# Copies of sampled keys on the activation engine, and a planner that counts on VectorE being held by GpSimd

## The chip, the cores and the metric

The kernel runs on one core of a Trainium2 chip. The engines work in parallel, each through its own queue of instructions in order, and wait for each other by semaphores: TensorE (PE, products), VectorE (DVE), ScalarE (ACT, the activation engine), GpSimd (POOL) and SyncE (SP, which here issues every transfer). On-chip data lies in SBUF (128 partitions) or in PSUM, where products land. The metric is the device time of one execution in microseconds; runs of the same kernel are given by their median.

## What is computed

Block-sparse attention, then a feed-forward layer with a rational function in its middle, cut from the reference:

```python
# q, k, v: (4, 8, 768, 64); 24 blocks of 32 rows; 3 sampled blocks of keys per query block
mask = np.abs(blk_i - blk_j) <= 1                      # the block and its neighbours
mask |= (blk_i == 0) | (blk_j == 0) | (blk_i == 23) | (blk_j == 23)
for qb in range(24):
    for kb in sampled_blocks[qb]:
        mask[qb*32:(qb+1)*32, kb*32:(kb+1)*32] = True
attn = softmax(where(mask, q @ k.T / 8, -1e9)); x = attn @ v      # (3072, 512)
h = x @ w_in                                                      # (3072, 2048)
P = a[0] + a[1]*h + a[2]*h*h + a[3]*h*h*h
Q = 1 + abs(b[0])*abs(h) + abs(b[1])*h*h
out = (P / (Q + 1e-6)) @ w_out                                    # (3072, 512)
```

So 22 of 24 query blocks look at eight blocks of keys (three neighbours, three sampled, the two edges), and the first and the last look at all. The weights come as 64-bit floats.

## The kernel before

**Tiles.** A query block with its eight heads is one step of attention. Keys and queries are scaled by a power of two and split into two halves of 16 bits, a high one (`high`, line 632 for keys) and a low one (`low`, VectorE, line 378), transposed on TensorE (line 660) and copied out of PSUM. For the first batch of the four the transposed keys of all 24 blocks stay in SBUF, in `kall`. For the later ones they go to a scratch in DRAM and come back by transfers, block by block.

**One step of attention.** Scores on TensorE (line 876), maxima with the mask's bias on VectorE (886), the negated maximum (915), exponentials on ScalarE (904), four transposes of the result (945), their copy out of PSUM (147, `pT`), products with the values (1002). Values come by transfers (lines 964 to 972). In the first batch the eight blocks of keys of a query block must lie side by side: the three neighbours are a slice of `kall`, and the two edge blocks (line 1072, once) and the three sampled ones (line 829, 128x256 elements each) are copied into one of two buffers `kxs`. The sampled blocks' numbers are data, so each step loads them into registers first (line 768). Before the change all of this copying is on GpSimd, three copies a step in 22 steps.

**The feed-forward part.** Groups of 256 rows (8 query blocks), and in them 16 units of two quarters of 128 columns. Per unit: first products on TensorE (lines 1113 to 1115), three ScalarE instructions that read PSUM (1120, 1124, 1134), VectorE's rational function (1127 to 1158) with ScalarE's logarithm and exponential in its middle (1141, 1144), second products (1169 to 1171).

**Decoding the weights.** In the first quarter of the program the 64-bit weights are loaded in 32 pieces (lines 422, 425). Each is converted (151 on GpSimd or 147 on ScalarE), packed by three VectorE instructions over SBUF (434, 437, 440), and then split into a high and a low part: input weights by ScalarE and GpSimd (`dw`, then line 498), output weights by ScalarE or GpSimd and GpSimd (line 451).

**The order.** All steps are entered in a list as `Op`s with an engine, a price in ns, the steps that they come after, and a priority. `issue` (lines 161 to 266) is a list scheduler that runs while the kernel is built: it keeps a modelled time `now` for each engine, takes the `Op` that could start first, and writes its instructions. So prices and starting rules set the order of every engine's queue, and nothing is reordered on the chip. An `Op` made with `among` names a home engine and may name others; another engine is taken if it could start earlier by more than `other[e]` (500 ns for VectorE, 534 for ScalarE, 243 for GpSimd). Where TensorE would wait long early in the program, `issue` writes filler products (line 159). The lines of the starting rule are these:

```python
196                    t = max([now[e], o.at[e]] + [s.ring.free[0][0] for s in o.takes])
197                    if e == SY:
198                        t = max(t, lanes[0])
199                    key = (max(t - slack, now[e]) + (0 if e == o.engs[0] else other[e]), o.prio, o.n)
```

Of the kernel before, what the change touches and what calls it, by code (L numbers as in the profile page):

```python
# [23 lines left out]
def kernel(  # L24
# [27 lines left out]
    nc = tc.nc  # L52
# [46 lines left out]
    OWN = {VE: 127, SC: 143, PO: 96}  # L99
    MARGIN = 17.0  # L100

    class Ring:


# [56 lines left out]
    def issue(ahead):  # L161
        def work_of(t, price, share):
            for x in (int(t / 3413), int(t / 3413) + 1):
                busy[x] = busy.get(x, 0.0) + share * max(0.0, min(t + price, (x + 1) * 3413) - max(t, x * 3413))

        def tick(t):
            nonlocal window, warm
            while window < int(t / 3413):
                share = busy.pop(window, 0.0) / 3413
                warm, window = share > (0.45 if warm else 0.85), window + 1  # L170

        todo = {e: [] for e in (VE, SC, PO, TE, SY, None)}
        now = dict.fromkeys(todo, 500.0)
        clock, dma, lanes = -1.0, 0.0, [0.0] * 8
        busy, window, warm = {}, 0, False
        for n, o in enumerate(plan):
            o.n, o.wait = n, len(o.after) + (o.behind is not None)
            for a in o.after:
                a.next.append(o)
            if o.behind:  # L180
                o.behind.next.append(o)
            if not o.wait:
                for e in o.engs:
                    todo[e].append(o)
        left = len(plan)
        fsh = 0.8
        other = {VE: 500, SC: 534.0, PO: 243.0}
        unit_of = {VE: nc.vector, SC: nc.scalar, PO: nc.gpsimd}
        slack, fend, f00, fgap = 21.0, 80000, 3000, 0
        while left:  # L190
            best = None
            for e, l in todo.items():
                for o in l:
                    if o.prio > clock + ahead or not all(s.ring.free for s in o.takes):
                        continue
                    t = max([now[e], o.at[e]] + [s.ring.free[0][0] for s in o.takes])
                    if e == SY:
                        t = max(t, lanes[0])
                    key = (max(t - slack, now[e]) + (0 if e == o.engs[0] else other[e]), o.prio, o.n)
                    if best is None or key < best[0]:  # L200
                        best = key, t, o, e
            if best is None:
                lim = [o for l in todo.values() for o in l]
                raise AssertionError([(o.eng, o.prio, o.run.__qualname__, [len(s.ring.free) for s in o.takes]) for o in lim][:40] + [clock])
            _, t, o, o.eng = best
            e = o.eng
            for x in o.engs:
                todo[x].remove(o)
            for s in o.takes:
                s.buf = s.ring.free.pop(0)[1]  # L210
            price = o.alt[e] if o.alt else o.price() if callable(o.price) else o.price
            o.start = t
            if isinstance(price, list):
                for ns, size in price:
                    t = max(t, lanes.pop(0) if e == SY else t) + ns
                    dma = max(dma, t + 650) + size / 225.0
                    if e == SY:
                        lanes.append(dma + 900)
                end = dma + 900
            elif e == TE:  # L220
                f0 = max(now[e], f00)
                while f0 < fend:
                    tick(f0)
                    f = 213 if warm else 427
                    if f0 + f + fgap > t:
                        break
                    fill()
                    work_of(f0, f, 1.0)
                    f0 += f
                tick(t)  # L230
                if now[e] < fend:
                    w = window
                    x0 = w * 3413
                    for _ in range(2):
                        if not warm or t - x0 < 700 or busy.get(w, 0.0) >= fsh * (t - x0):
                            break
                        fill()
                        work_of(t, 213, 1.0)
                        t += 213
                if not warm:  # L240
                    price *= 2 if price > 1100 or price < 500 else 1.8
                work_of(t, price, o.work)
                end = t = t + price
            else:
                end = t = t + price
            now[e] = t
            o.end = end
            o.run(unit_of[e]) if o.alt else o.run()
            if o.unit is not None:
                clock = max(clock, o.unit)  # L250
            for s in o.uses:
                s.left -= 1
                s.end = max(s.end, end + (0 if isinstance(price, list) else 200))
                if not s.left:
                    s.ring.free.append((s.end, s.buf))
                    s.ring.free.sort(key=lambda f: f[0])
            for x in o.next:
                if x.behind is not o:
                    for y in x.engs:
                        lat = MARGIN if isinstance(price, list) else OWN.get(e, 0) if y == e else LAT.get((e, y), 160) + MARGIN  # L260
                        x.at[y] = max(x.at[y], end + lat)
                x.wait -= 1
                if not x.wait:
                    for y in x.engs:
                        todo[y].append(x)
            left -= 1
# [348 lines left out]
    def rest(b, w, j, d, o_scale, sc, prio, before):  # L615
        first = b == 0
        t, g = units[j]
# [18 lines left out]
        def low():  # L636
            split16(d["ld"], sc[0], d["hl"], w, None)

        o = Op(among("k", PO, po=671, ve=396, sc=613) if w == 0 else among("K", PO, po=914, ve=600), 0, high, [o_scale, o_ld], prio, takes=[s_hl], uses=[s_ld])
        o = Op(VE, 663 if w == 0 else 800, low, [o], prio, uses=[s_ld, s_hl])  # L640
        if w == 1:
            def store():
# [153 lines left out]
    def attention(b, j, prio):  # L796
# [15 lines left out]
        for m, x in enumerate(xs):  # L812
            def one(m, x):
# [6 lines left out]
                if near and n > 1:  # L820
                    deps += [o for t in range(NCH) for o in k_evac[b, t]]
                    kslots = s_kall
                elif near:
                    s_kx = Slot(r_kx)

                    def copies():
                        rows = sampled_rows(x, mybir.EngineType.Pool)
                        for r in range(NR):
                            nc.gpsimd.tensor_copy(out=kxs[:, s_kx.buf, r].rearrange("p h r -> p (h r)"), in_=kall[:, bass.ds(rows[r], 1)].rearrange("p o h r -> p (o h r)"))

                    a = Op(PO, 1500, copies, [o_setup, chain["edges"]], p - 1, takes=[s_kx], uses=s_kall)
                    deps.append(a)
                    kslots = [s_kx] + s_kall
                else:
                    s_kg = Slot(r_kg)

                    def load():
                        kg, ks, = kgs[s_kg.buf], kv[b][0]
                        flat = kg.rearrange("p s h r -> p s (h r)")
                        if n > 1:  # L840
                            nc.sync.dma_start(out=flat, in_=ks[m * NS:(m + 1) * NS].rearrange("b p c -> p b c"))
                            return
                        nc.sync.dma_start(out=flat[:, 0:3], in_=ks[i - 1:i + 2].rearrange("b p c -> p b c"))
                        if h["new"]:
                            nc.sync.dma_start(out=flat[:, 3 + NR:], in_=ks[0:NB:NB - 1].rearrange("b p c -> p b c"))
                        rows = sampled_rows(x)
                        for r in range(NR):
                            nc.sync.dma_start(out=flat[:, 3 + r], in_=ks[bass.ds(rows[r], 1)].rearrange("o p c -> p (o c)"))

                    def price():  # L850
                        h["new"] = fresh("k", x, s_kg)
                        if n > 1:
                            return [(475, 524288)]
                        l = [(475, 196608)] + ([(475, 131072)] if h["new"] else [])
                        return l + [(860, 65536), (560, 65536), (560, 65536)]

                    a = Op(SY, price, load, [o_setup] + k_done[b], p - 1.95, takes=[s_kg], uses=[s_scr[b]], behind=chain.get("kg"))
                    chain["kg"] = a
                    deps.append(a)
                    kslots = [s_kg]  # L860
# [458 lines left out]
```

## Time and profile before

| | |
|---|---|
| median of 3 runs | 892.88 us (891.15 to 894.04) |
| the profiled execution | 894.15 us |
| its span, first to last instruction | 892.0 us |
| TensorE busy | 828.4 us (93%), 10328 products |
| VectorE busy | 743.9 us (83%), 1824 instructions |
| ScalarE busy | 653.1 us (73%), 1379 instructions |
| GpSimd busy | 157.0 us (18%), 188 instructions |
| DMA, one queue | 146.29 MB, 65.8% of 16 engines' span |

The profile is of one execution. A line such as L829 is a line of the kernel as it is printed above. "Busy" is the union of an engine's instructions; an engine's waits for semaphores, its register work and its transfers' issues aren't in it. The stage table gives busy time for each engine in a stretch of the span, with TensorE's granted clock (1.00 is full) and the share of time in which the 16 DMA engines were busy. GpSimd's spans are rough.

### The profile page before, as it was taken

To read this page: it belongs to the slowest core of one execution; us is meant where nothing else is said; L and a number is where in the kernel's file an instruction comes from. 1 tells how busy PE (TensorE), PEld (TensorE's weight loads), DVE (VectorE), ACT (ScalarE), POOL (GpSimd) and SP (SyncE) were. 2 spreads that over 40 slices of the span, in tenths; PEclk is the share of its full clock that TensorE was granted. 3 is DMA by queue.
4 is the path that set the end of the run, shared out by engine and by line. 5 is a ranking of instruction groups with operands and counts; after the bars stand their busy time and mean duration, and the time that the engine had idled before them with its cause. 6 is when DMAs were issued, how large, how long until landed. Compare 5 with 4: busy or idle time off the path is not lost.

```text
span 892.0 us, 27246 instructions
## 1 busy us (share of the span) xinstructions
PE 828.4 (93%) x10328; PEld 644.8 (72%) x10328; DVE 743.9 (83%) x1824; ACT 653.1 (73%) x1379; POOL 157.0 (18%) x188
## 2 busy tenths in 40 slices
PE   8988586776999999989999999999999999999997
PEld 3555365565778888777887788878888787788885
DVE  5668999979999888869877788988888887788885
ACT  6668666794788787778876887798758587767563
POOL 2434755736420000100000000200000000000000
PEclk9999798688899999999999999999999999999999
DMA  7799788875776976589655975699557556740000
GB/s 204 188 180 219 175 185 172 183 203 161 188 175 160 250 211 155 149 201 240 176 144 149 264 203 161 156 236 240 152 151 183 145 158 161 174 113 25 1 25 24
DMA packets 238482, 148.02 MB, mean 166 GB/s; under 512 B 16016, under 2 KB 222736, under 8 KB 238352
## 3 DMA queue, kind: packets, MB, share of 16 engines
q1 hardware_dynamic: 238352, 146.29, 65.8%
q8 instruction: 82, 1.34, 0.7%
q14 instruction: 48, 0.39, 0.2%
HBM read 128.92 MB, written 11.01 MB: 157 GB/s over the span
## 4 chain that ended last, share of the span: by engine, by line
PE 61%; DVE 8%; ACT 3%; DMA 3%; SPq 2%; issue 1%; ACTq 0%; DVEq 0%
PE ph L1113 8%; PE acc L1169 8%; PE acc L1171 8%; PE acc L1170 8%; PE ph L1114 7%; PE ph L1115 7%; PE av L1002 5%; PE pt L945 4%; PE sp L876 4%; DMA ld<-in_k_dram 1%; DVE gh L1148 1%; DVE ab L1137 1%; PE sp L733 1%; DVE tt L1154 1%; PE sp L1048 1%
## 5 line engine op out<-in xcount | busy, mean ns | idle before, releaser
L1113 PE MATMUL ph<-xh,wi 128*128 128x256 f16 x768 | 213.2, 278 | 3.8 <-DVE tt L1130 2.6
L1115 PE MATMUL ph<-xh,wi 128*128 128x256 f16 x768 | 212.0, 276 | 2.4 <-POOL wi L498 2.4
L1114 PE MATMUL ph<-xl,wi 128*128 128x256 f16 x768 | 212.0, 276 | 1.0 <-DVE xl L1060 1.0
L904 ACT ACTIVATE pr<-pr,st,cq 128x256 f32<-128x256 f32 x224 | 132.2, 593 | 61.0 <-DVE st L915 54.2
L1169 PE MATMUL acc<-wo_h,gh 128*128 128x512 f32 x384 | 164.9, 429 | 0.0
L1171 PE MATMUL acc<-wo_h,gl 128*128 128x512 f32 x384 | 154.7, 403 | 7.3 <-DVE gl L1158 6.6
L1170 PE MATMUL acc<-wo_l,gh 128*128 128x512 f32 x384 | 154.1, 401 | 1.2 <-POOL wo_l L451 1.2
L1120 ACT ACTIVATE sq<-ph,fc 128x512 f32<-128x512 f32 x96 | 65.3, 680 | 60.2 <-PE ph L1115 59.7
L1137 DVE SCALAR_TENSOR_TENSOR ab<-sq,absb,ab 128x512 f32<-128x512 f32 x96 | 74.1, 772 | 34.3 <-ACT ab L1134 34.0
L151 POOL TENSOR_SCALAR hlq<-ldq,scq 128x512 f16<-128x512 f32 x24 | 23.2, 968 | 445.2 <-DVE scq L352 239.5
L1113 PEld LDWEIGHTS <-wi 128*128 128x128 f16 x768 | 76.2, 99 | 32.2 <-issue 16.5
L886 DVE CUSTOM_DVE_ANT_1 pr<-sp,bias 128x256 f32<-128x256 f32 x224 | 84.6, 418 | 13.8 <-PE sp L876 13.4
L1171 PEld LDWEIGHTS acc<-wo_h,gl 128*128 128x128 f32 x384 | 73.6, 192 | 26.6 <-DVE gl L1158 9.3
L1148 DVE SCALAR_TENSOR_TENSOR gh<-tt,par,rr 128x512 fp32r<-128x512 f32 x96 | 74.9, 780 | 17.1 <-PE acc L1170 13.1
L945 PE MATMUL pt<-ident,pr 128*128 128x128 f32 x448 | 77.1, 294 | 11.8 <-ACT pr L904 7.7
L1115 PEld LDWEIGHTS <-wi 128*128 128x128 f16 x768 | 76.1, 99 | 13.8 <-POOL wi L498 2.9
L1169 PEld LDWEIGHTS acc<-wo_h,gh 128*128 128x128 f32 x384 | 73.9, 192 | 15.7 <-issue 1.2
L945 PEld LDWEIGHTS pt<-ident,pr 128*128 128x128 f32 x448 | 67.4, 206 | 24.7 <-ACT pr L904 10.1
L1170 PEld LDWEIGHTS acc<-wo_l,gh 128*128 128x128 f32 x384 | 73.9, 192 | 14.0 <-POOL wo_l L451 1.8
L1114 PEld LDWEIGHTS <-wi 128*128 128x128 f16 x768 | 76.1, 99 | 9.1 <-issue 1.1
L1002 PE MATMUL av<-vg,pT 128*32 128x64 f32 x3584 | 75.1, 226 | 4.7 <-ACT pT L147 2.5
L1002 PEld LDWEIGHTS av<-vg,pT 128*32 128x32 f32 x3584 | 57.1, 112 | 29.5 <-issue 8.9
(140 smaller groups left out, 1669.3 us busy)
## 6 DMA issues: line engine op xcount, KB each, us to landing
vg<-in_v_dram SPq DMA_DIRECT2D x312, 64.0 KB, 3.3
vg<-in_v_dram SPq DMA_DIRECT2D x88, 192.0 KB, 4.1
vg<-in_v_dram SPq DMA_DIRECT2D x24, 512.0 KB, 5.2
kall<-ks SPq DMA_DIRECT2D x52, 192.0 KB, 2.9
kall<-ks SPq DMA_DIRECT2D x156, 64.0 KB, 2.0
ld<-in_k_dram SPq DMA_DIRECT2D x36, 256.0 KB, 5.5
wl<-in_moe_w_in_dram SPq DMA_DIRECT2D x32, 256.0 KB, 4.8
wl<-in_moe_w_out_dram SPq DMA_DIRECT2D x16, 512.0 KB, 4.1
```

The costliest lines, as they stand in the source:

```text
L886: nc.vector.tensor_tensor_reduce(out=prs[x][:, g].rearrange("p (s r) -> p s r", r=BLK), in0=h["sp"][:, g].rearrange("p (s r) -> p s r", r= ...
L904: nc.scalar.activation(out=prs[x][:, g], in_=prs[x][:, g], func=AF.Exp, scale=Q["c"], bias=st[:, 6 + g:7 + g], accum_out=total if n == 1 e ...
L945: nc.tensor.transpose(pp[:, jj * P:(jj + 1) * P], cols, ident)
L1002: nc.tensor.matmul(av[rows, g], pT[:, 2 * g + kt, rows] if plain else pT[:, 2 * g + kt, pa_, rows], vf[:, g * HG + h4, kt * D:(kt + 1) * D ...
L1113: nc.tensor.matmul(o, wh, xh[:, :, cc], start=(cc == 0), stop=False)
L1114: nc.tensor.matmul(o, wh, xl[:, :, cc], start=False, stop=False)
L1115: nc.tensor.matmul(o, wl, xh[:, :, cc], start=False, stop=(cc == NCC - 1))
L1137: nc.vector.scalar_tensor_tensor(out=d["ab"], in0=d["sq"], scalar=absb[:, 1:2], in1=d["ab"], op0=ALU.mult, op1=ALU.add)
L1148: nc.vector.scalar_tensor_tensor(out=d["gh"], in0=d["tt"], scalar=par[:, 0:1], in1=d["rr"], op0=ALU.add, op1=ALU.mult)
L1169: nc.tensor.matmul(acc[:, t], ghs, wo_h[:, f], start=(new and e == 0), stop=False)
L1170: nc.tensor.matmul(acc[:, t], ghs, wo_l[:, f], start=False, stop=False)
L1171: nc.tensor.matmul(acc[:, t], gls, wo_h[:, f], start=False, stop=(last and e == 1))
```

## The change

Three things change. The three copies of sampled keys of a step, and the register loads ahead of them, move from GpSimd to ScalarE, with a price of 1100 ns in place of 1500. The high halves of keys (`high`, for keys of all batches) have ScalarE as home, and GpSimd and VectorE as the others. And the planner notes, after each `Op` on GpSimd, its modelled start and end in `held`; a VectorE `Op` that would start in between, and whose function isn't one of a list of those that read PSUM, starts later by half of what is left.

```diff
+    READS_PSUM = {"maxima", "cubic3", "weigh", "evac_high", "evac_low", "largest", "add", "copy", "evac", "whole"}
+    HELD = 0.5
...
+        held = 0.0, 0.0
...
+                    if e == VE and held[0] <= t < held[1] and o.run.__name__ not in READS_PSUM:
+                        t += HELD * (held[1] - t)
                     key = (max(t - slack, now[e]) + (0 if e == o.engs[0] else other[e]), o.prio, o.n)
...
             now[e] = t
+            if e == PO:
+                held = o.start, end
...
-        o = Op(among("k", PO, po=671, ve=396, sc=613) if w == 0 else among("K", PO, po=914, ve=600), 0, high, [o_scale, o_ld], prio, takes=[s_hl], uses=[s_ld])
+        o = Op(among("k", SC, po=671, ve=396, sc=613) if w == 0 else among("K", PO, po=914, ve=600), 0, high, [o_scale, o_ld], prio, takes=[s_hl], uses=[s_ld])
...
-                        rows = sampled_rows(x, mybir.EngineType.Pool)
+                        rows = sampled_rows(x, mybir.EngineType.Activation)
                         for r in range(NR):
-                            nc.gpsimd.tensor_copy(out=kxs[:, s_kx.buf, r]..., in_=kall[:, bass.ds(rows[r], 1)]...)
-
-                    a = Op(PO, 1500, copies, [o_setup, chain["edges"]], p - 1, takes=[s_kx], uses=s_kall)
+                            nc.scalar.copy(out=kxs[:, s_kx.buf, r]..., in_=kall[:, bass.ds(rows[r], 1)]...)
+
+                    a = Op(SC, 1100, copies, [o_setup, chain["edges"]], p - 1, takes=[s_kx], uses=s_kall)
```

What it does to the queues shows at two places. The first is ScalarE's queue at the first sampled blocks, where exponentials (`pr`) follow each other with the query's evacuation (`qa`) and the evacuations of transposed results (`pT`) between them. Line numbers of the changed kernel are 3 to 8 higher (904 is 912, 147 is 150, 737 is 745, 829 is 837). Before:

```order
L904 ACTIVATE pr,sm<-pr,st,cq 128x256 x2
L147 ACTIVATE wi<-wl 128x512
L147 ACTIVATE pT<-pt 128x512
L904 ACTIVATE pr,sm<-pr,st,cq 128x256 x2
L737 ACTIVATE qa<-sp 128x2x512
```

The same place now, from the second block's last copy:

```order
L837 COPY kx<-kall 128x256
L776 TENSOR_LOAD ix
L837 ISA
L837 COPY kx<-kall 128x256
...
L745 ACTIVATE qa<-sp 128x2x512
L912 ACTIVATE pr,sm<-pr,st,cq 128x256 x4
L776 TENSOR_LOAD ix
L837 ISA
L837 COPY kx<-kall 128x256
```

Each block now brings a register load, three register instructions (`ISA`) and three copies into this queue; the third block's stand ahead of the evacuation of the query and of the first exponentials, and the fourth's behind four exponentials instead of beside two.

The second is GpSimd's queue at the first group of input weights: `wi<-wl` is the conversion of a piece, `dw<-wi` its scaling and `wi<-dw,wi` its low part, `hlq` a query's high half. Before, from the last copies that stand ahead of the group's scaling:

```order
L768 TENSOR_LOAD ix
L829 ISA
L829 COPY kx<-kall 128x256
...
L151 TENSOR_SCALAR dw<-wi,scw 128x512 x3
L498 TENSOR_TENSOR wi<-dw,wi 128x512 x3
L151 TENSOR_SCALAR dw<-wi,scw 128x512
```

Now, from the copies of the two edge blocks, which stay on GpSimd:

```order
L1080 COPY kx<-kall 128x512 x2
L154 TENSOR_SCALAR hlq<-ldq,scq 128x8x64
L154 TENSOR_SCALAR wi<-wl 128x512 x4
L154 TENSOR_SCALAR dw<-wi,scw 128x512 x3
L506 TENSOR_TENSOR wi<-dw,wi 128x512 x3
```

The decode of this group follows the edge blocks' copies at once, with all four conversions on GpSimd, where 13 blocks of copies stood between.

## Rows read from the trace of the kernel before

**Rows 1.** Stage table: busy us and count by engine, clock, DMA share, GB/s

```profile
27.00:82.00 55.00, 47.48 (x902) 28.49 (x901) 38.12 (x138) 37.20 (x97) 28.62 (x53) 0.97 0.91 192
82.00:104.00 22.00, 13.87 (x240) 10.09 (x237) 18.81 (x44) 17.79 (x41) 13.94 (x16) 0.95 0.99 239
104.00:201.00 97.00, 73.92 (x985) 56.80 (x986) 88.31 (x194) 71.45 (x153) 51.58 (x56) 0.82 0.78 180
201.00:258.00 57.00, 48.01 (x558) 36.67 (x557) 56.97 (x123) 35.89 (x71) 29.24 (x23) 0.88 0.70 176
258.00:892.00 634.00, 621.99 (x7516) 501.68 (x7514) 525.12 (x1270) 474.52 (x983) 26.38 (x27) 1.00 0.61 157
```

**Rows 2.** Timeline, GpSimd and VectorE: start us, duration us, engine, line, operation

```profile
92.08 2.82 POOL L498 TENSOR_TENSOR wi<-dw,wi 128x512 f16<-128x512 f32 x2 [1.21 <-ACT wi L147]
97.90 3.20 POOL L498 TENSOR_TENSOR wi<-dw,wi 128x512 f16<-128x512 f32 x2
101.08 1.13 POOL L151 TENSOR_SCALAR hlq<-ldq,scq 128x512 f16<-128x512 f32 x1
...
92.36 1.53 DVE L437 SCALAR_TENSOR_TENSOR dw<-wl,dw 128x512 int32<-128x512 int32 x1
...
100.01 0.14 DVE L724 TENSOR_SCALAR cq<-cq 128x1 f32<-128x1 f32 x1
...
101.64 0.73 DVE L1130 SCALAR_TENSOR_TENSOR tt<-ph,fc,tt 128x512 f32<-128x512 f32 x1
...
112.77 0.69 DVE L437 SCALAR_TENSOR_TENSOR dw<-wl,dw 128x512 int32<-128x512 int32 x1
```

**Rows 3.** One line's or tile's instructions: ns min/median/max, waits (us, times)

```profile
L829 POOL COPY kx<-kall x66: 392/400/952, 27.3 to 182.3; 128x256 f16 x66
...
  PE sp L876: 11.1, 8
...
L768 POOLq TENSOR_LOAD <-ix x22: 725/730/946, 26.2 to 175.3; - x22
```

**Rows 4.** Stage table for the tile `kx`: TensorE's reads, then GpSimd's copies

```profile
104.00:201.00 97.00, 5.58 (x144) 15.16 (x24) 0.82 0.78 180
```

**Rows 5.** Timeline of VectorE, instructions that run beside copies and high halves

```profile
102.30 0.80 DVE L1154 SCALAR_TENSOR_TENSOR tt<-tt,par,ab 128x512 f32<-128x512 f32 x1
...
129.97 0.88 DVE L1127 TENSOR_TENSOR tt<-tt,sq 128x512 f32<-128x512 f32 x1
...
153.28 1.17 DVE L378 SCALAR_TENSOR_TENSOR hl<-ld,sc,hl 128x512 f16<-128x512 f32 x1 [0.59 <-POOL hl L151]
...
179.10 1.06 DVE L1151 SCALAR_TENSOR_TENSOR ab<-ab,gh 128x512 f32<-128x512 f32 x1
...
182.78 0.62 DVE L434 TENSOR_SCALAR wi<-wi 128x512 int32<-128x512 int32 x1
```

**Rows 6.** Groups of TensorE: busy us, mean ns, idle before and its releaser

```profile
L1115 PE MATMUL ph<-xh,wi 128*128 128x256 f16 x768 | 212.0, 276 | 2.4 <-POOL wi L498 2.4
...
L159 PE MATMUL acc<-ident 128*128 128x512 f16 x180 | 49.1, 401 | 1.7 <-DVE ident L93 1.7
```

**Rows 7.** Groups of ScalarE up to 290 us

```profile
L904 ACT ACTIVATE pr<-pr,st,cq 128x256 f32<-128x256 f32 x70 | 41.3, 593 | 19.7 <-DVE st L915 19.6
...
L297 ACT ACTIVATE absb<-par 128x2 f32<-128x2 f32 x1 | 0.2, 204 | 3.9 <-DMA par<-in_moe_b_dram 3.9
```

**Rows 8.** Timeline of GpSimd at the first sampled blocks

```profile
27.35 2.27 POOL L829 COPY kx<-kall 128x256 f16 x6
```

**Rows 9.** Groups of GpSimd up to 290 us

```profile
L451 POOL TENSOR_TENSOR wo_l<-dw,wo_h 128x512 fp32r<-128x512 f32 x16 | 23.4, 1461 | 18.3 <-ACT wo_h L147 17.8
L498 POOL TENSOR_TENSOR wi<-dw,wi 128x512 f16<-128x512 f32 x16 | 22.7, 1436 | 4.7 <-ACT wi L147 4.7
```

**Rows 10.** Transfers issued: count, KB each, median us to landing

```profile
vg<-in_v_dram SPq DMA_DIRECT2D x312, 64.0 KB, 3.3
vg<-in_v_dram SPq DMA_DIRECT2D x88, 192.0 KB, 4.1
```

More of the change, by code (lines that the diff above doesn't have):

```diff
@@ L826, in copies @@
                     def copies():
-                        rows = sampled_rows(x, mybir.EngineType.Pool)
+                        rows = sampled_rows(x, mybir.EngineType.Activation)
                         for r in range(NR):
-                            nc.gpsimd.tensor_copy(out=kxs[:, s_kx.buf, r].rearrange("p h r -> p (h r)"), in_=kall[:, bass.ds(rows[r], 1)].rearrange("p o h r -> p (o h r)"))
-                    a = Op(PO, 1500, copies, [o_setup, chain["edges"]], p - 1, takes=[s_kx], uses=s_kall)
+                            nc.scalar.copy(out=kxs[:, s_kx.buf, r].rearrange("p h r -> p (h r)"), in_=kall[:, bass.ds(rows[r], 1)].rearrange("p o h r -> p (o h r)"))
+                    a = Op(SC, 1100, copies, [o_setup, chain["edges"]], p - 1, takes=[s_kx], uses=s_kall)
                     deps.append(a)
```

## The prediction

> **What bounds the kernel now.** I started from the page's busy shares (TensorE 93%, VectorE 83%, ScalarE 73%), but they are averages over stages with different limits, so the stage table is the view that counts [rows 1]. It shows four regimes. From 27 to 104 us the DMA engines are 91% and 99% busy: transfers set the pace. From 104 to 201 us VectorE is busy 88.31 of 97 us and ScalarE 71.45. From 201 to 258 us VectorE is busy 56.97 of 57 us. From 258 us to the end TensorE is busy 621.99 of 634 us, at the full clock. The copies of the change lie in the first 201 us. They can move the end only by bringing the start of the last regime forward or back: from about the 42nd first-layer half on (lines 1113 to 1115), TensorE's orders before and after agree but for a few swaps.
>
> So the question is how long the prelude lasts, and in its part from 104 to 258 us VectorE is the scarce engine. Some of its busy time is no work. Beside GpSimd's 2.82 us of line 498 an instruction of line 437, with two inputs in SBUF, is recorded at 1.53 us; without GpSimd it takes 0.69 [rows 2]. One that reads PSUM, line 1130, keeps its 0.73 us while GpSimd's line 151 runs [rows 2].
>
> **The change, part by part.**
>
> *Key copies leave GpSimd.* They are 66, at a median of 400 ns [rows 3], in 22 blocks of three; 15.16 us of them lie from 104 to 201 us [rows 4]. What VectorE gets back is not that time but only the holding. I went through the VectorE instructions that overlap such a copy and took from each the usual duration of its line where GpSimd is silent. From 82 to 201 us there are 16, the first at 102.30 and the last at 182.78; a typical one, line 1127 at 129.97, takes 0.88 us [rows 5], 0.19 more than the 0.69 of such a width. Together they lose 2.6 us. Holds before 82 us lie in the transfer-bound stage and count nothing. **Term 1: -2.6 us.**
>
> *High halves of keys.* The planner may now put them on ScalarE first. Of 24, GpSimd did 23; it keeps 13, ScalarE has 10 and VectorE one. Two VectorE instructions in the prelude were held by one, 1.17 us at 153.28 and 1.06 at 179.10 [rows 5]; against 0.69 alone [rows 2] that is 0.85. **Term 2: -0.8 us.** In exchange VectorE gets one high half and one weight conversion. Neither shows on VectorE before; the nearest row is line 434, of the same width, 0.62 us beside a copy [rows 5]. Between nothing (in the transfer-bound stage) and 1.5 us I take two at 0.4. **Term 3: +0.8 us.**
>
> *GpSimd's queue gets shorter.* TensorE stands idle 2.4 us in front of line 1115 for GpSimd's line 498 [rows 6]. Without copies ahead of it this comes sooner, but TensorE isn't the scarce engine there: from 0 to 2.4 us, and I take a fifth. **Term 4: -0.5 us.**
>
> *Copies arrive on ScalarE.* The trace has no ScalarE copy of 128x256. It lies above an instruction of 2 elements, 204 ns, and below one of 256 with its exponential, 593 ns [rows 7]. Half-way is 0.4 us, so three make 1.2 and 22 blocks 26 us (13 to 39). Ten high halves instead of one, less three copies of weights that leave ScalarE, are six more at the 0.6 of [rows 7], 4 us. Together 30 us. ScalarE's idle time from 27 to 201 us is 174 - 126.4 = 47.6 us [rows 1], so the load fits and leaves 17. Each block also loads three indices into registers, 730 ns on GpSimd's queue [rows 3]. There they were hidden: six copies with such a load between them took 2.27 us, 0.38 apiece [rows 8]. If ScalarE hides none, 22 x 0.73 = 16 us more, and its slack is gone. I take hidden, as the queue that was seen did it.
>
> In sentences by themselves: the Trainium skill ("DMA: Bandwidth & Descriptors", Latency and other measured facts) gives loads of this kind a floor of about 600 ns. Unhidden, that is an estimated 13 us of ScalarE, and speaks against the change; the row's 730 ns is longer, and decides.
>
> ScalarE's queue also takes over a wait. The copies of a block wait for the scores that used its buffer two blocks earlier; GpSimd stood 11.1 us in 8 such waits [rows 3]. Behind them on ScalarE are queued the query's evacuation (line 737), exponentials (904) and evacuations before the value product (147); TensorE's transposes and VectorE's sums wait for those. 15 of the 22 blocks stand before the first output product, most of them in the transfer-bound stage, which covers them; ScalarE waits 19.6 us for line 915 as it is [rows 7], and copies fill part of that. From 0 to 11 us, and I take the low end. **Term 5: +0.5 us.**
>
> *The planner's new rule.* In the plan a VectorE instruction over SBUF starts later by half of what is left of GpSimd's instruction, so that one over PSUM may go first. Most holding comes from lines 451 and 498, 1.46 and 1.44 us long [rows 9], and they stay on GpSimd. I looked for the rule's effect in the new order: of the six instructions behind each of the 16 output-weight decodes (line 440), 40 of 96 read PSUM before and 29 of 96 now. The plan doesn't do there what the rule is for. **Term 6: 0 us**, with some 4 on either side.
>
> *More filler.* 201 warm-up products of line 159 in place of 180, which took 49.1 us [rows 6]. They stand at the start, where TensorE waits for transfers, so they cost nothing; with real work behind all 21 it would be 21 x 0.27 = 6 us.
>
> **Sum.** -2.6 - 0.8 + 0.8 - 0.5 + 0.5 + 0 = -2.6; the small holds that I left out (under 0.04 us each) bring it to about -3. The profiled execution took 894.15 us, 2.15 more than its span of 892.0; it becomes 891.15. The median of the runs, 892.88, lies 1.27 lower, so the forecast is **889.9 us**, -0.3%.
>
> **Rivals.**
>
> *ScalarE's queue becomes the bound (slower).* Place: the sampled blocks from 104 to 201 us, where ScalarE is busy 71.45 of 97 [rows 1]. Seven blocks (8.4 us), their register loads (5.1) and six halves (3.6) bring it to 88.6, as full as VectorE. From there neither engine has slack: each wait at the head of ScalarE's queue delays exponentials, and VectorE stands idle for them. Price: the 11.1 us of waits that GpSimd absorbed, less the 3 gained, 894.15 + 8.1 - 1.27 = **901 us**. For it: in 14 of the 22 blocks the first copy still waits for TensorE. Against: the planner knew these waits when it placed the copies, at 1100 ns a block.
>
> *Weights come earlier (faster).* In the queue of transfers the first group of input weights is complete behind 4 loads of values instead of 7. One is 192 + 3 x 64 KB [rows 10], three are 1.15 MB, and at 192 GB/s [rows 1] 6 us. If the first layer starts that much sooner and VectorE can fill the time, the prelude ends as much earlier on top: **884 us**. Against: from the ninth output piece on both orders stand within 1 MB of each other.
>
> *The rule doesn't do what it says (no change).* With 11 fewer PSUM instructions beside the decode more of VectorE is held. A hold of line 437 is 0.84 us at most [rows 2]; half of the 11 at half of that is 2.3 us, which eats most of the gain: **892.2 us**. The rule is also too wide: line 724, 128x1 in SBUF, takes 0.14 us within GpSimd's 3.20 [rows 2], so it isn't held, and yet the planner delays it. The Trainium skill ("SBUF — State Buffer", Who interferes with whom) says that an instruction with a single SBUF input, outside the two-port modes, doesn't contend; by that, and line 724 agrees, the rule moves such instructions for nothing.
>
> **How the numbers follow.** Forecast's mechanism 46%, 887 to 892.7 (31 faster by over 0.3%, 15 inside). ScalarE's queue 28%, slower. Weights earlier 10%, faster. Rule without effect 16% (11 inside, 5 slower). Faster 31 + 10 = 41%, within 0.3% 15 + 11 = 26%, slower 28 + 5 = 33%. 0.3%, 2.7 us, is about what a measurement of this kernel can tell from no change. The range reaches from the weights' case with the rule working as well (884 - 3) to the queue's case with some register loads unhidden (901 + 3): 881 to 904.
>
> **What would show it.** Right: from 104 to 201 us ScalarE's busy time rises by some 12 us, line 904 gets no new wait of more than 5 us in all, and TensorE's unbroken stretch starts about 3 us earlier. Wrong towards slower: new idle time of VectorE that ends with line 904 or 147, gaps between ScalarE's copies, a copy well above 0.4 us, VectorE still saturated after 258 us. Wrong towards faster: the first products of line 1113 come clearly before 82 us, or lines 437 and 440 keep near 0.69 us beside GpSimd's decode.

## The result, and the profile after

The changed kernel takes 890.48 us (median of 10 runs, 888.51 to 892.74), the kernel before 894.04 beside it (10 runs, 891.15 to 898.44): a ratio of 0.9947, 95% interval 0.9927 to 0.9967 (ratios here are of mean times, so they can differ a little from those of the medians). It is faster, by 0.5%; the forecast was 889.9 us, -0.3%. The profiled execution of the changed kernel took 892.74 us with a span of 890.9, the slowest of its ten, and this is worth keeping in mind below; its copy e12, run later, gave 0.992. Line numbers have moved: 147 and 151 are now 150 and 154, and lines from 335 to 1171 have numbers higher by 8 (437 is 445, 904 is 912, 1113 is 1121).

The stage table after, in the columns of [rows 1] (stretch; busy us and count of TensorE, its weight loads, VectorE, ScalarE, GpSimd; granted clock, DMA share, GB/s):

```profile
27.00:82.00 55.00, 46.01 (x718) 27.39 (x716) 33.98 (x103) 40.32 (x107) 13.45 (x16) 0.97 0.91 186
82.00:104.00 22.00, 16.16 (x260) 9.42 (x261) 20.73 (x66) 19.36 (x47) 11.36 (x12) 0.81 0.43 138
104.00:201.00 97.00, 78.61 (x1204) 60.71 (x1203) 90.23 (x219) 84.93 (x199) 34.91 (x32) 0.90 0.85 205
201.00:258.00 57.00, 49.02 (x592) 37.35 (x591) 55.06 (x124) 41.58 (x86) 26.31 (x22) 0.94 0.77 188
258.00:890.00 632.00, 620.12 (x7444) 499.93 (x7442) 520.84 (x1259) 472.80 (x977) 19.58 (x22) 0.99 0.61 157
```

From 104 to 201 us the load has changed sides: ScalarE 84.93 us busy where it was 71.45, GpSimd 34.91 where it was 51.58. VectorE is as full as before and slightly fuller. From 201 to 258 us, where VectorE was busy 56.97 of 57 us, it now has a gap of 1.94. The DMA engines, at 0.99 from 82 to 104 us before, are at 0.43: that stage is no longer one of transfers. TensorE's mean clock (1.00 is the full 2.4 GHz) is 0.90 for 0.82 and 0.94 for 0.88 in the two VectorE stages, with 78.61 us busy for 73.92 in the first of them, and 0.81 for 0.95 from 82 to 104 us.

The copies on ScalarE, and the loads ahead of them (ns min/median/max, first and last start, shape; then what their engine waited for, us and times):

```profile
L837 ACT COPY kx<-kall x66: 387/401/430, 26.9 to 180.5; 128x256 f16 x66
...
  PE sp L884: 1.6, 2
...
L776 ACTq TENSOR_LOAD <-ix x22: 695/702/893, 25.3 to 176.9; - x22
```

A copy takes 401 ns, and never more than 430, where on GpSimd it took 392 to 952 [rows 3]. The waits for scores shrank from 11.1 us in 8 to 1.6 us in 2. From 0 to 290 us, busy us, mean ns of one, and the idle time ahead by releaser, the same copies and the exponentials:

```profile
L912 ACT ACTIVATE pr<-pr,st,cq 128x256 f32<-128x256 f32 x72 | 42.4, 591 | 6.8 <-DVE st L923 6.6
L837 ACT COPY kx<-kall 128x256 f16 x66 | 22.0, 402 | 2.8 <-PE sp L884 1.6 <-DVE kall L152 0.8 <-issue 0.4
```

All 66 copies make 22.0 us, less than 66 x 0.40, since three in a row overlap. The exponentials' wait for VectorE fell from 19.6 us [rows 7] to 6.6. Copies fill part of it, and the new order takes away part: run e6 below, which has the new order and the copies on GpSimd, shows 11.9.

So far this reads as the forecast had it. The next view does not. It lists what ended VectorE's idle time from 27 to 258 us (us in total, times, longest). Before:

```profile
DVE pr L886 <- PE sp L876: 6.6, 4, 3.5
DVE wi L434 <- POOL wi L151: 5.4, 4, 2.4
DVE scq L340 <- PE sp L335: 3.3, 1, 3.3
DVE sm L1029 <- ACT pr L904: 2.6, 2, 1.9
DVE wi L434 <- ACT wi L147: 2.5, 3, 1.6
DVE dw L434 <- ACT dw L147: 2.2, 1, 2.2
...
DVE hl L378 <- POOL hl L151: 1.2, 2, 0.6
```

After:

```profile
DVE wi L442 <- POOL wi L154: 9.4, 4, 3.7
DVE ab L1145 <- ACT ab L1142: 6.0, 4, 2.8
DVE wi L442 <- ACT wi L150: 4.0, 4, 1.7
DVE scq L348 <- PE sp L343: 2.4, 2, 1.5
DVE pr L894 <- PE sp L884: 2.3, 4, 1.0
```

VectorE used to wait for TensorE's scores; it now waits for ScalarE (lines 1142 and 150) and for GpSimd's conversions of input weights, whose share grew although GpSimd has less to do. These four waits lie from 35 to 54 us, where transfers set the pace, and the conversions themselves stood behind the weights' transfers. GpSimd's conversions up to 290 us (busy us, mean ns, idle time ahead), before and after:

```profile
L151 POOL TENSOR_SCALAR wi<-wl 128x512 f32<-128x512 f32 x6 | 5.4, 894 | 10.2 <-DMA wl<-in_moe_w_in_dram 10.2
```

```profile
L154 POOL TENSOR_SCALAR wi<-wl 128x512 f32<-128x512 f32 x6 | 4.0, 664 | 29.1 <-DMA wl<-in_moe_w_in_dram 29.1
```

So GpSimd was ready earlier and the weights were not. Summed by releaser over all rows of the view, VectorE waited 12.0 us for TensorE, 6.6 for GpSimd and 9.0 for ScalarE before, and 6.3, 10.2 and 13.2 after. The total went from 27.6 to 29.7 us. In e12, the same kernel once more, the three are 5.7, 8.5 and 10.5.

Two sums of my own are used below. Of VectorE: for each of its instructions that overlaps one on GpSimd, the excess over the median duration of the same line and tiles where GpSimd is silent; summed from 82 us, where the prediction begins to count, to 258 us, that is its **held time**, 31.2 us before and 24.9 after. (The expectation of e2 has 28 us for it before; by this definition it is 31.2.) Of the order: the **lead**, by which the square (line 1120) of a first-layer half starts earlier than in the profile of before; there are 96 of them. Both are from one execution each. Two executions of the changed kernel (after, and e12) differ by 2.2 us in held time, 3.4 in VectorE's idle time from 82 to 258 us, up to 2.7 in the waits by releaser and some 3 to 5 in leads, so only differences beyond that are read.

### The profile page after: what moved, and what is told of

Its sections match the earlier page's. It is cut to its first block, busy times and chain, and to the rows that moved or that the text cites. A ratio compares the mean times of both kernels' runs of the same rounds, so it can differ in the third digit from the quotient of the medians.

```text
span 890.9 us, 27280 instructions
## 1 busy us (share of the span) xinstructions
PE 833.8 (94%) x10349; PEld 646.3 (73%) x10349; DVE 737.1 (83%) x1826; ACT 676.7 (76%) x1451; POOL 109.9 (12%) x114
## 4 chain that ended last, share of the span: by engine, by line
PE 65%; DMA 9%; DVE 9%; ACT 7%; SPq 6%; issue 3%; ACTq 0%; POOL 0%; DVEq 0%; POOLq 0%
PE acc L1177 9%; PE acc L1178 8%; PE acc L1179 8%; PE ph L1121 8%; PE ph L1122 7%; PE ph L1123 7%; PE av L1010 5%; PE sp L884 4%; PE pt L953 4%; DMA vg<-in_v_dram 3%; DMA ldq<-in_q_dram 2%; ACT pr L912 1%; ACT scrap L392 1%; DMA wl<-in_moe_w_out_dram 1%; SPq L980 1%
## 5 line engine op out<-in xcount | busy, mean ns | idle before, releaser
L1156 DVE SCALAR_TENSOR_TENSOR gh<-tt,par,rr 128x512 fp32r<-128x512 f32 x96 | 72.7, 757 | 14.0 <-PE acc L1178 13.4
L1178 PEld LDWEIGHTS acc<-wo_l,gh 128*128 128x128 f32 x384 | 73.9, 193 | 13.5 <-POOL wo_l L459 1.7
L154 POOL TENSOR_SCALAR hlq<-ldq,scq 128x512 f16<-128x512 f32 x24 | 21.4, 892 | 504.9 <-DVE scq L360 306.6
```

The lines of the kernel that those rows point to most:

```text
L1156: nc.vector.scalar_tensor_tensor(out=d["gh"], in0=d["tt"], scalar=par[:, 0:1], in1=d["rr"], op0=ALU.add, op1=ALU.mult)
L1178: nc.tensor.matmul(acc[:, t], ghs, wo_l[:, f], start=False, stop=False)
```

## The experiments

The change has three parts: the copies' engine (C), the high halves' home (K) and the planner's rule (H). Each makes the planner lay out all the work anew, so each run changes an engine and an order at once. Two runs separate those.

**The engine without the order, and the order without the engine.** Both take the copy's code alone and leave what the planner books for it.

```diff
 e5, in the kernel before:
-  rows = sampled_rows(x, mybir.EngineType.Pool) ... nc.gpsimd.tensor_copy(...)
+  rows = sampled_rows(x, mybir.EngineType.Activation) ... nc.scalar.copy(...)
   a = Op(PO, 1500, copies, ...)
 e6, in the kernel after:
-  rows = sampled_rows(x, mybir.EngineType.Activation) ... nc.scalar.copy(...)
+  rows = sampled_rows(x, mybir.EngineType.Pool) ... nc.gpsimd.tensor_copy(...)
   a = Op(SC, 1100, copies, ...)
```

> The copies run on ScalarE, but the planner still books them on GpSimd at 1500 ns, so that every other instruction keeps the order of the kernel before; each copy stands in ScalarE's queue where the planner wrote it out. If the gain is VectorE's release from the copies' holds and the copies fill ScalarE's idle time, 2 to 4 us less than before. If ScalarE's queue becomes the bound where nobody planned for it, 4 to 10 us more than before. If the gain is the new order alone, within 1 us of before.

> The changed kernel's plan with the copies run on GpSimd: the order of all else is that of the changed kernel, and the planner believes the copies on ScalarE. If the gain is the order (weights and their decode earlier), this is 2 to 4 us below before. If it is the engine, this is within 1 us of before or slower, since GpSimd gets 33 us of copies that the plan doesn't know of in front of its decode.

Measured: e5 897.2 us against 897.24, ratio 1.0006 (0.9979 to 1.0034); e6 893.09, ratio 0.9964 (0.9935 to 0.9994). In the old order moving the copies and nothing else is worth nothing, and the interval leaves no room for the 2 to 4 us; the new order with the copies back on GpSimd is faster, by 0.4%, with an interval that ends just below 1. From e6 to the changed kernel (0.9947, 0.992) the engine alone may be worth nothing or the whole forecast gain: the intervals overlap. What VectorE waits for in e5 from 27 to 258 us:

```profile
DVE pr L886 <- PE sp L876: 6.9, 3, 3.5
DVE scq L340 <- PE sp L335: 4.9, 1, 4.9
DVE wi L434 <- ACT wi L147: 4.7, 4, 1.8
DVE wi L434 <- POOL wi L151: 4.1, 3, 2.2
DVE sm L1029 <- ACT pr L904: 3.4, 2, 2.9
DVE xl L1060 <- ACT xh L147: 2.5, 2, 1.6
DVE dw L434 <- ACT dw L147: 2.2, 1, 2.2
DVE ab L1137 <- ACT ab L1134: 1.6, 2, 0.8
```

The waits for GpSimd fall, from 6.6 to 4.6 us, and those for ScalarE rise from 9.0 to 15.4: several of the awaited instructions of lines 147 and 1134 stand close behind a block of copies. Held time fell by 1.5 us, to 29.7, and VectorE's idle time from 82 to 258 us rose by 1.8. The relief is there, and so is its price. The first square starts 3.2 us later than before, as if part of the price were paid before 104 us, where I had said that transfers cover it; but 3.2 us is no more than two executions differ by.

e6 keeps the order of after and has 6.0, 7.2 and 11.6 us of waits for TensorE, GpSimd and ScalarE. The 11.6 is near after and e12 with the copies on the other engine, so in the new order the waits for ScalarE are not the copies' own. The fall of held time is: e6 has 29.7 us, after 24.9 and e12 27.1. The busy times say the same without a sum of mine, since VectorE does the same 1826 instructions in the same order in all three. Of e6, after and e12:

```profile
PE 834.0 (94%) x10349; PEld 647.0 (73%) x10349; DVE 742.9 (83%) x1826; ACT 657.1 (74%) x1385; POOL 144.1 (16%) x180
PE 833.8 (94%) x10349; PEld 646.3 (73%) x10349; DVE 737.1 (83%) x1826; ACT 676.7 (76%) x1451; POOL 109.9 (12%) x114
PE 830.4 (94%) x10349; PEld 645.0 (73%) x10349; DVE 739.0 (83%) x1826; ACT 677.2 (76%) x1451; POOL 111.0 (13%) x114
```

With the copies on GpSimd VectorE needs 3.9 to 5.8 us longer for the same work. The relief that the forecast counted on is real in the new order.

**Each copy twice**, to weigh a copy on either engine.

```diff
   for r in range(NR):
       nc.gpsimd.tensor_copy(...)      # e7, in before;  e8, in after: nc.scalar.copy(...)
+      nc.gpsimd.tensor_copy(...)      # e8: nc.scalar.copy(...)
```

> The kernel before with each of the 66 copies made twice on GpSimd, unplanned: GpSimd's busy time goes up by some 33 us. If holding is what a copy costs, VectorE loses another 2.6 us in the bound stage: 2 to 4 us slower than before. If GpSimd's queue is what it costs (decode behind copies), 5 to 12 us slower. If copies on GpSimd cost nothing, within 1 us.

> The changed kernel with each of the 66 copies made twice on ScalarE, unplanned: 66 x 0.40 = 26 us more of ScalarE, 11 of it from 104 to 201 us, where it was busy 84.9 of 97 us. If ScalarE has slack there, within 2 us of the changed kernel. If its queue is near being the bound, 4 to 10 us slower than the changed kernel.

Measured: e7 907.16 us, ratio 1.0109 (1.0068 to 1.015), 9.9 us more than before. e8 904.57, ratio 1.0088 (1.0059 to 1.0118); the changed kernel at 0.992 to 0.9947 of the same 897.24 would be 890.1 to 892.5, so its second copies cost 12 to 14.5 us, more than the 4 to 10 I had put on a queue near its bound. Copies of e7, then of e8, from 0 to 290 us:

```profile
L830 POOL COPY kx<-kall 128x256 f16 x66 | 34.5, 522 | 4.1
L829 POOL COPY kx<-kall 128x256 f16 x66 | 32.6, 494 | 8.7 <-issue 3.4 <-PE sp L877 3.1 <-PE pt L946 2.1
```

```profile
L838 ACT COPY kx<-kall 128x256 f16 x66 | 26.7, 405 | 2.1
L837 ACT COPY kx<-kall 128x256 f16 x66 | 26.4, 400 | 3.5 <-issue 2.3 <-DVE kall L152 0.8 <-PE sp L885 0.4
```

On GpSimd 34 us of added copies (67.1 less the 33.3 of before) cost 9.9 us, on ScalarE 31 us (53.1 less 22.0) cost 12 to 14.5. With intervals of some 3 us on either side the two are not told apart, and the orders differ; that ScalarE is the cheaper place for a copy isn't shown. In e7 VectorE's waits for GpSimd grow from 6.6 to 17.6 us and its held time by 2.4; in e8 its waits for ScalarE grow from 13.2 to 26.5 us and its held time doesn't grow (22.5 us). On both engines the price is mostly waiting, and little of it holding.

**The parts, in all combinations.** e1 is C, e2 H, e3 K; e4 is C and K (the rule's factor set to 0), e9 H and K, e10 C and H, e12 the change again.

```diff
 e1:  the copies' hunk alone        e2:  READS_PSUM, HELD, held alone
 e3:  -among("k", PO, ...)  +among("k", SC, ...)
 e4, in after:  -HELD = 0.5  +HELD = 0.0
 e9, in after:  the copies' hunk reversed      e10, in after:  e3 reversed
```

> The kernel before with the copies of sampled keys alone on ScalarE, planned there at 1100 ns; high halves of keys and the planner's rule as before. If the gain is VectorE's release from copies and GpSimd's shorter queue, this has most of it: 2 to 4 us less than before, and VectorE's holds from 104 to 201 us near 10 us instead of 14. If the gain comes from the new rule, this is within 1 us of before. If it takes all three parts together (an accident of the order), it may be slower than before by up to 5 us.

> The kernel before with the planner's rule alone (half of what is left of GpSimd's instruction); copies and high halves stay on GpSimd. If the rule moves PSUM instructions under GpSimd's work, holds fall from 28 us (82 to 258 us) to 23 or less and the time by 3 to 5 us. By the prediction's count of the order the rule does nothing: within 2 us of before, holds within 3 us.

> The kernel before with ScalarE as home of the keys' high halves alone. By the prediction's second and third terms this is worth nothing (-0.8 and +0.8 us): within 2 us of before. If moving these halves is what brings the gain, 3 us or more less.

> The changed kernel with the planner's rule at nothing (factor 0 in place of 0.5); copies and high halves on ScalarE. If the rule brings nothing, this is as fast as the changed kernel, 3 to 5 us below before. If the rule brings the gain, it is within 1 us of before or slower.

> The changed kernel without its first part: copies of sampled keys on GpSimd as before, high halves at home on ScalarE and the planner's rule at 0.5. So far each of these two alone was worth 7 us and both stand in the change. If parts add up, this is 10 us or more below before. If each is only another draw of the order, 3 to 8 us below before.

> The changed kernel without its second part: copies on ScalarE and the planner's rule, high halves at home on GpSimd as before. Copies alone came out 4 us slower and the rule alone 7 us faster. If parts add up, 3 us below before. If copies on ScalarE cost what the order can't hide, at or above before.

> The changed kernel unaltered, on the same chip as the three others, with another profiled execution. If the stumble at 359 us belongs to this order of the queues, it is there again within 1 us of its place, and the time is 3 to 5 us below before. If it was an accident of one execution, it is absent.

Measured, with the waits of VectorE by releaser (27 to 258 us, summed as above), its held time and its idle time (82 to 258 us), the lead at 331 us, and TensorE's idle time from 331 to 598 us:

| kernel | median us | ratio (95%) | VectorE waits for PE / GpSimd / ScalarE | held | VectorE idle | lead at 331 | TensorE idle, 331 to 598 |
|---|---|---|---|---|---|---|---|
| before | - | 1 | 12.0 / 6.6 / 9.0 | 31.2 | 11.9 | 0 | 6.6 |
| H (e2) | 888.26 | 0.992 (0.9892-0.9949) | 16.8 / 5.7 / 6.1 | 29.8 | 8.6 | 1.8 | 4.1 |
| K (e3) | 886.62 | 0.9921 (0.9893-0.9948) | 7.3 / 4.0 / 7.0 | 30.0 | 6.3 | 3.9 | 2.0 |
| H, K (e9) | 884.45 | 0.9888 (0.986-0.9916) | 10.6 / 5.5 / 3.0 | 29.5 | 2.8 | 4.3 | 1.3 |
| C (e1) | 900.04 | 1.0047 (1.0019-1.0074) | 14.1 / 6.5 / 10.8 | 28.0 | 12.2 | -9.3 | 6.4 |
| C, H (e10) | 887.8 | 0.992 (0.9888-0.9952) | 7.3 / 7.9 / 13.8 | 27.5 | 10.2 | 3.1 | 4.2 |
| C, K (e4) | 886.08 | 0.9917 (0.9882-0.9951) | 8.3 / 10.0 / 11.2 | 30.2 | 9.8 | 0.4 | 3.8 |
| C, H, K (after) | 890.48 | 0.9947 (0.9927-0.9967) | 6.3 / 10.2 / 13.2 | 24.9 | 10.0 | 5.8 | 6.6 |
| C, H, K (e12) | 888.01 | 0.992 (0.9891-0.9949) | 5.7 / 8.5 / 10.5 | 27.1 | 6.6 | 8.9 | 6.1 |
| engine without order (e5) | 897.2 | 1.0006 (0.9979-1.0034) | 11.8 / 4.6 / 15.4 | 29.7 | 13.7 | -4.7 | 4.8 |
| order without engine (e6) | 893.09 | 0.9964 (0.9935-0.9994) | 6.0 / 7.2 / 11.6 | 29.7 | 7.8 | 3.7 | 7.7 |

Read in pairs of planned kernels that differ by C, the copies' move makes nothing faster: none to C +0.5%, H to CH no difference, K to CK no difference, HK to the full change +0.3 to 0.6%. H and K alone bring 0.8% each, and together 1.1%, which isn't told apart from either alone. HK, with the copies left on GpSimd, beats both kernels: its six runs took 882.21 to 887.55 us, those of the change in the same session 885.98 to 890.37. It has the shortest waits for ScalarE (3.0 us), and nearly as much held time as before (29.5 us). In the five with the copies planned on ScalarE VectorE's waits for that engine are 10.5 us or more, in the four of the first nine rows with them planned on GpSimd 9.0 or less.

Held time alone doesn't order the kernels: the four rows with the least of it are the full change's two, CH and C, and C is slower than before. Held and idle time of VectorE added up do order the prelude. Where the sum is 35 us or less (HK, e12, after) the lead at 331 us is 4.3 to 8.9 us; from 36.3 to 40.0 (K, e6, CH, H, CK) it is 3.9 to 0.4; above that (C 40.2, before 43.1, e5 43.4) there is none, and e7, at 52.0, is 18.1 us behind. So what VectorE lost past 82 us, whether held or idle, goes with how late the prelude ends, although this comes from single executions and C, 9.3 us behind, fits in sign only. The last column is of another stretch and leaves the prelude out; e5 keeps the order of before and has 4.8 there for 6.6, so some 2 us of it are spread. VectorE's waits of e9, against those of after above:

```profile
DVE pr L894 <- PE sp L884: 5.4, 5, 2.2
DVE wi L442 <- POOL wi L154: 4.7, 3, 2.9
DVE ab L1145 <- ACT ab L1142: 2.5, 1, 2.5
```

**Where the lead goes after the prelude.** At 331 us, in the steady stretch, the changed kernel was 5.8 us ahead; at 875 us only 1.1 (in e12 8.9, then 5.6). e9 goes from 4.3 to 11.9, e3 from 3.9 to 8.9. So the full change has the earliest end of the prelude of all, and gives much of it back; in the prelude alone C on top of H and K costs nothing. The stretch from 331 to 598 us in the stage table, columns as above. Of before:

```profile
331.00:598.00 267.00, 260.38 (x3361) 209.87 (x3359) 220.71 (x558) 210.66 (x445) 18.12 (x19) 0.99 0.73 185
```

Of after:

```profile
331.00:598.00 267.00, 260.37 (x3320) 209.75 (x3309) 217.40 (x555) 209.81 (x442) 12.22 (x14) 0.98 0.74 185
```

Of e3:

```profile
331.00:598.00 267.00, 265.02 (x3431) 213.46 (x3424) 223.09 (x578) 216.03 (x460) 19.58 (x19) 1.00 0.75 192
```

Of e9:

```profile
331.00:598.00 267.00, 265.67 (x3430) 214.63 (x3429) 225.61 (x586) 217.25 (x461) 15.30 (x19) 1.00 0.75 193
```

TensorE isn't unbroken there. It stands idle 6.6 us before and after, 2.0 in e3, 1.3 in e9, and that difference, 4.6 and 5.3 us, is most of what e3 and e9 gain in these 267 us (4.8 and 8.5 us of lead from 331 to 598). Idle time isn't all: after has as much of it as before and still loses 4.3 us of lead. The granted clock in the rows is likely another part, 0.98 after, 0.99 before and 1.00 in e3 and e9: a hundredth of it over some 260 us of products is an estimated 2.6 us, which goes the right way in all three without adding up exactly. The largest stumble of after, in the timeline (start us, duration us, then the idle time ahead and its releaser):

```profile
358.06 1.36 SPq L711 DMA_DIRECT2D ldq<-in_q_dram  x2
...
361.95 0.63 ACT L392 ACTIVATE scrap<-ldq 128x512 f16<-128x512 f32 x1 [5.91 <-DMA ldq<-in_q_dram]
...
362.73 0.48 PE L343 MATMUL sp<-ident,mxq 128*128 128x128 f32 x1 [3.36 <-ACT scrap L392]
```

A query tile's load is issued at 358.06; ScalarE starts on the tile 3.9 us later, after standing idle for 5.91 us, and TensorE waits 3.36 us for the tile's maximum. In e12 the same wait is there again, 3.3 us sooner by the clock, in a run that is 3.1 us further ahead at 331 us:

```profile
359.45 0.47 PE L343 MATMUL sp<-ident,mxq 128*128 128x128 f32 x1 [3.13 <-ACT scrap L392]
```

e6, of the same order, has 3.43 us of it at 364.9 us. So the stumble belongs to the order and not to one execution. From 355 to 375 us the clock is 1.00 in the kernel before, first, and 0.83 with the stumble, second:

```profile
355.00:375.00 20.00, 19.19 (x244) 15.78 (x244) 16.51 (x46) 14.53 (x28) 1.82 (x2) 1.00 0.66 169
```

```profile
355.00:375.00 20.00, 16.64 (x184) 13.24 (x182) 12.08 (x37) 9.79 (x18) 1.82 (x2) 0.83 0.66 165
```

e11 orders these later query loads one step earlier, and leaves the queues up to about 290 us as they are in after:

```diff
-  o_ld = Op(SY, ..., load, (), prio - 1, ...)
+  o_ld = Op(SY, ..., load, (), prio - (1 if prio < 0 else 2), ...)
```

> The changed kernel with the load of each later query tile planned one place earlier (priority minus 2 in place of minus 1); the queues are the same up to about 290 us. In the profile of the changed kernel TensorE stood 3.4 us at 359 us for a query's maximum, whose load was issued at 358, and its clock was granted at 0.83 in that stretch. If the gain of the prelude is given back at such loads, the time falls by 3 to 6 us against the changed kernel and the 3.4 us are gone. If it is lost anyway (the next transfer is then late), within 1 us of the changed kernel.

Measured: 887.34 us, ratio 0.9908 (0.9879 to 0.9937); e12 beside it 888.01, 0.992. Not told apart; the 3 to 6 us that were expected if such loads were the loss aren't there beside e12. TensorE's groups from 331 to 870 us, of e12 and of e11:

```profile
L1010 PE MATMUL av<-vg,pT 128*32 128x64 f32 x2240 | 45.7, 222 | 2.0 <-ACT pT L150 2.0
L343 PE MATMUL sp<-ident,mxq 128*128 128x128 f32 x13 | 3.9, 302 | 5.1 <-ACT scrap L392 5.1
```

```profile
L953 PE MATMUL pt<-ident,pr 128*128 128x128 f32 x280 | 46.8, 288 | 2.7 <-ACT pr L912 2.6
L1010 PE MATMUL av<-vg,pT 128*32 128x64 f32 x2240 | 45.6, 222 | 4.1 <-ACT pT L150 4.1
L343 PE MATMUL sp<-ident,mxq 128*128 128x128 f32 x13 | 3.6, 278 | 0.6 <-DVE st L894 0.6
```

The wait is gone from line 343, 5.1 to 0.6 us, and 2.1 us of it are back in front of line 1010 and 2.7 in front of 953, both now behind ScalarE. Removing one stumble moved the idle time to other places of the order: from 331 to 598 us e11 has 8.5 us of it for 6.1 in e12, at a clock of 1.00 for 0.99.

## Why the prediction was right, and where it was not

The time, its sign and its range were right, and part of the reason. That 889.9 us came so near to 890.48 is luck: the high halves and the rule were each worth some 7 us alone where nothing was booked, and the queue of term 5 cost 6.4 us of waits in the old order where 0.5 was. By the steps of the prediction:

- **What bounds the kernel.** The stages were read rightly, and VectorE's lost time from 82 to 258 us does go with the end of the prelude. The prelude ended earlier, as the forecast had it, by 5.8 and 8.9 us of lead at 331 us where 3 were forecast; 3.7 of it is there with the copies on GpSimd (e6). One sentence failed: that the copies "can move the end only by bringing the start of the last regime forward or back". The table puts 1.3 to 7.7 us of TensorE's idle time into the last regime, by order. That is more than the whole forecast gain, and I had passed over it because 621.99 of 634 us looked full [rows 1].
- **Terms 1 and 2, held time.** In the old order the copies' move takes away 1.5 us of it (e5), in the new one 2.6 to 4.8 (e6 against e12 and after), around the 2.6 of term 1. The term was sized about rightly, and the step from it to the time failed: in e5 VectorE's idle time grew by about as much as its held time fell, and e9 has 29.5 us of held time for 31.2 and is 1.1% faster. In the new order the step may hold; e6 and the changed kernel aren't told apart.
- **Term 3 and the high halves.** With term 2 I booked K at nothing, -0.8 + 0.8. Alone it brought 0.8%: VectorE's idle time from 27 to 258 us goes from 28.8 to 21.5 us, and TensorE's in the steady stretch from 6.6 to 2.0. I had looked only at what a half on GpSimd holds. But VectorE's waits for these halves were just 1.2 us (line 378), and what shrank most is its waiting for TensorE, 12.0 to 7.3: here too most of it is another order of everything.
- **Term 4, GpSimd's shorter queue.** Forecast as a small gain. The 2.4 us of TensorE's idle time that it was made of are gone (line 1123 has 0.0); e6 has lost them too and e5 keeps 1.9, so this is the order's. VectorE's waits for GpSimd grew from 6.6 to 10.2 us (8.5 in e12), nearly all for conversions that waited for transfers, in the stage that the prediction counts at nothing.
- **Term 5, the copies on ScalarE.** The price of one, 0.4 us, was right (401 ns); the 22 register loads, 702 ns each, left no gap ahead of the copies and were hidden, as assumed. That load reads here 702 ns, longer than the 600 that the Trainium skill ("DMA: Bandwidth & Descriptors", Latency and other measured facts) gives as its floor, and the 13 us of cost estimated from that figure did not come. ScalarE's busy time from 104 to 201 us rose by 13.5 us, forecast 12. But +0.5 us for the queue was mis-sized: VectorE waits 6.4 us longer for ScalarE in the old order (e5); in the new one 1.5 to 4.2, but e6, with 2.6, has that too. "I take the low end" of 0 to 11 us had no row behind it; the copies' own waits, which the bound was made of, went almost to nothing, and in e5 the cost came from the instructions behind them.
- **Term 6, the planner's rule.** Taken at 0 with 4 on either side; alone it is worth 0.8%, 6.5 us. It did not do it by what it is for: alone it leaves held time at 29.8 us of 31.2. With C it repairs a bad order (1.0047 to 0.992), on top of C and K it brings nothing (0.9917 to 0.992 and 0.9947). So it seems to act as another order; no run separates its aim from the order that it makes.
- **The rivals.** ScalarE's queue as the bound was real as a mechanism and some 30 us of copies away as a result: e5 shows it eating the gain, e8 what it costs when the load doubles. Whether e1 loses its 0.5% by it isn't shown: VectorE waits there only 1.8 us longer for ScalarE. Of "weights come earlier" its first half happened: the first square starts at 76.7 us instead of 85.1. The lead wasn't kept, the fifth half starts 18.6 us later than before; the planner put more sampled attention ahead of it, 44 exponentials and 65 copies where 38 and 56 stood. By 331 us the order is ahead again. The rule without effect was right on its effect on holding, and wrong on the time.

**What stays open.** No run shows why one order stumbles less than another. Part of it is TensorE's idle time and clock from 331 to 598 us, and e11 shows that taking away its largest cause isn't enough. Whether the engine alone brings time in the new order is not shown: e6 and the changed kernel would need more runs side by side. The eight combinations come from one planner at one setting each; that H or K would bring 0.8% under another setting isn't shown.

## What to carry to other kernels

Where a planner lays out the work, an edit to it is two changes, an engine and an order, and here the second was the larger: without moving a copy, the new orders of e2, e3, e6 and e9 brought 0.4 to 1.1%, and the engine alone brought nothing in the old order. Issue the moved work on the new engine with the old bookings, and the other way round, before believing a mechanism. Time saved on an engine by less contention counts only if that engine then has something to do: add up its held and its idle time in the stage that it bounds, and list what ends its idle time before and after, by releaser. Count the instructions that stand behind the moved ones in their new queue, not only the moved ones' own waits. A last stage at 98% is not unbroken: its few per cent of idle time may be as large as the gain that is being looked for.

## What the runs showed of the hardware

A copy of 128x256 16-bit elements takes 401 ns on ScalarE, 387 to 430 over all 66, and three in a row 1.00 to 1.03 us; on GpSimd the same copy takes 400 ns at the median [rows 3]. Seven of the 66 in the kernel before overlap nothing on VectorE and take 400 to 401; the others take up to 952. The holding goes both ways: with these copies on GpSimd VectorE is busy 742.9 us for the 1826 instructions that take it 737.1 and 739.0 with the copies on ScalarE. A load of an index into registers, 702 ns at the median, ran on ScalarE's queue without a gap in front of the copies behind it. TensorE's clock fell to 0.83 in the 20 us that held one stumble of 3.4 us, and stood at 1.00 in the same 20 us without it.
